# The first thirty microseconds of a fused conv and MLP kernel: longer TensorE warm-up, first input chunk in four transfers, later weight loads, one scaling on GpSimd

## The chip, the cores and the metric

The kernel runs on one NeuronCore of a Trainium2 chip. The metric is device time in microseconds (us), lower is better. Times are given as the median of several executions. One of them is profiled, and its span is about 1.7 us shorter than its time, because the profile counts from the first to the last instruction. Engines in the profile: PE is TensorE's matmul, PEld its weight load, DVE is VectorE, ACT is ScalarE, POOL is GpSimd, SP is the sync engine, which only issues transfers here.

## The reference

```python
# attention-like part: per head a causal convolution with 7 softmaxed taps
w = softmax(weight, axis=-1)                       # [8 heads, 7]
x_pad = concat([zeros(B, 6, D), x], axis=1)        # B=8, S=4096, D=192
conv[b, s, h, g] = sum_k w[h, k] * x_pad[b, s + k, h, g]
# MLP part, on 32768 tokens
h = conv @ w_in                                    # 192 -> 2048
g = h * sigmoid(beta * h)
out = g @ w_out                                    # 2048 -> 192
```

Inputs and output are float32. The kernel computes `silu(beta * h)` with `beta` as the activation's scale, and divides `w_out` by `beta` once at the start ("scaling of w_out").

## The kernel before

The tokens come in 32 stages of 2 x 512 tokens (two halves of the batch, `h = 0, 1`). In a stage, 16 blocks (`u`) each compute 128 hidden channels: six hidden matmuls, one silu on ACT, and output matmuls for earlier blocks. Chunk c's rows are loaded, cast to bf16, transposed so that channels lie on partitions, and convolved. For chunks 2 and on, the convolution runs on DVE and the transposes are DMAs. Chunk 0 is different: PE transposes it and convolves it with diagonal matrices (16 tap matmuls), because nothing else is ready yet. Chunk 1 is split between PE (`conv1`) and DVE.

The parts that the change touches (cuts marked with `...`):

```python
    def load_x(dst, t0):                      # two transfers of 384 KB, both h in each
        for i in range(2):
            t = t0 + i * 2 * BLK
            nc.sync.dma_start(
                out=dst[:, i].rearrange("q h b d -> q h (b d)"),
                in_=x_v[0, t : t + 2 * BLK, :, :].rearrange("(q b) h d -> q h (b d)", b=2))

    load_x(x0, 0)                             # chunk 0
    load_x(x1, TOK)                           # chunk 1
    for i in range(NW - 1):
        load_w_out(i)                         # w_out in quarters
    load(2); load_w_out(NW - 1); load(3)
    ...
    load_w_in(0)                              # w_in by quarters, GpSimd queue, cast to bf16 on the way
    ...
    def fill(n, cols=TOK):                    # matmuls of zeros: they only keep TensorE busy
        for _ in range(n):
            nc.tensor.matmul(pf[:, 0, 0:cols], zeros[:, 0:128], zeros[:, 0:cols], ...)

    fill(5)
    nc.tensor.matmul(pw, sel..., e8, ...)     # spreads the softmaxed taps over partitions
    fill(1, 384)
    for b in range(NB):                       # rows of chunk 0 to bf16, by token block
        cast_rows(nc.vector.tensor_copy, x0b, x0, b)
    ...
    hold = setup.tile([1, 1], BF16)           # GpSimd waits here for the first cast ...
    nc.gpsimd.tensor_copy(hold, x0b[0:1, 0, 0, 0, 0:1])
    for i in range(1, NW):
        load_w_in(i)                          # ... and issues the other w_in quarters then
    for b in range(NB):                       # PE transposes, ACT evacuates, fills between
        transposes(pt, x0b, b); nc.scalar.copy(tokens(xt0, b), pt)
        ...
    # diag = ident * cw (DVE); 16 diag taps (PE); 5 taps of the third channel group (DVE)
    ...
    CONV1 = {4: (0, 2), 5: (2, 4), 6: (4, 6), 7: (6, K)}   # chunk 1's PE taps in blocks 4..7
    first_work = {                            # DVE work of stage 0, by block; None = next conv step
        4: [None, lambda: scale_w_out(1), None],
        5: [None],
        7: [conv1_evac, lambda: scale_w_out(2), lambda: rows_of(2), None],
        8: [None, lambda: scale_w_out(3)],
        9: [None], 10: [None]}
```

`rows_of(2)` casts chunk 2's rows on DVE and starts their transposes. DVE works strictly in this order.

## Time and profile before

| | before |
|---|---|
| median, range (3 runs) | 693.16 us, 693.14 to 694.39 |
| profiled run: time, span | 692.46 us, 690.7 us |
| last row cast of chunk 0 ends | 6.13 us |
| first conv tap | 7.83 us |
| first silu | 14.31 us |
| second hidden block of stage 1 | 33.01 us |
| from there to the last hidden block, and to the end | 644.7 us, 13.1 us |

The second hidden block of stage 1 is a good marker. In every profile of this study except e7's and e9's (which move work into stage 1), the time from it to the start of the last stage (stage 31) is 626.29 to 626.31 us, and from there to the start of the last hidden block it is 18.37 to 18.38 us. Everything that differs lies before it or after the last hidden block.

From the page of the kernel before, its span and the busy time of the engines (busy us, share of the span, instructions):

```profile
span 690.7 us, 24335 instructions
PE 684.2 (99%) x11311; PEld 518.1 (75%) x11311; DVE 526.6 (76%) x466; ACT 579.1 (84%) x531; POOL 6.8 (1%) x18
```

PE is the limit of the whole. The reader should not conclude that the opening is also PE-bound. The timeline of the kernel before says otherwise. Its columns are start in us, length in us, engine, line, operation, output<-input, how many instructions were merged, and in brackets the idle time before and what ended it:

```profile
1.26 2.31 PE L228 MATMUL ph<-zeros 128*128 128x512 bf16 x5 [1.26 <-DVE warm L178]
...
4.29 0.74 DVE L233 CAST x0b<-x 128x384 bf16<-128x384 f32 x2 [1.78 <-DMA x<-in_x_dram]
...
5.35 0.78 DVE L233 CAST x0b<-x 128x384 bf16<-128x384 f32 x2 [0.32 <-DMA x<-in_x_dram]
...
7.83 3.04 PE L279 MATMUL ph<-xt,diag 128*128 128x512 f32 x7
...
10.71 1.79 PE L279 MATMUL pb<-xt,diag 128*128 128x512 f32 x7
...
14.31 6.45 ACT L425 ACTIVATE g<-ph,beta 128x1024 bf16<-128x1024 f32 x6
```

Seven taps took 3.04 us and the next seven 1.79 us. The same operation at two speeds is TensorE's clock. Single taps start about 427 ns apart up to the fifth interval (the first, 561 ns, excepted); the sixth is 378 ns, and from then on about 230 ns. The Trainium skill ("TensorE: Matmul & The Clock Gate", Part 1) describes a clock gate that lets half speed through until one free-running window of 3.4 us was busy, with 426.7 and 215.7 ns at N=512; the trace agrees with the first figure and shows about 230 ns for these fp32 taps. This trace holds no record of the first grant, so here the clock had to be read from the spacing.

The chain of waits of the kernel before, followed back from stage 1 (start us, length us, what ran; only the pieces that matter):

```profile
14.31 2.12 ACT g L425 x2
...
22.33 0.68 DVE ct L396
...
23.75 0.96 DVE w_out_s L313
24.71 1.20 DVE xb L106 x2
...
28.49 0.87 DVE w_out_s L313
29.35 1.21 DVE ct L335
...
30.59 1.29 DVE ct L335
...
31.92 0.61 PE ph L417 x4
```

From 22.33 us on the chain is DVE alone: conv1's evacuation, a scaling, chunk 2's casts, conv steps. PE waits for its end, at 31.92 us.

### The profile page before, as it was taken

What the parts mean: (1) busy time and instruction counts of PE and PEld (TensorE: products, weight loads), DVE (VectorE), ACT (ScalarE), POOL (GpSimd) and SP (SyncE); (2) the same over time, 40 slices, a digit from 0 to 9 for tenths busy, and PEclk for the clock granted to TensorE, in tenths of its full rate; (3) what the DMA queues carried; (4) which work ended last, traced back from release to release, by engine and by line L of the source; (5) the groups of instructions that cost most, each with busy time, mean ns of one, the idle gap of its engine ahead of it and who ended that gap; (6) DMA issues with size and microseconds to landing.
All of it is one profiled execution on the core that took longest, in us unless ns stands there. A gap on an engine that the chain in (4) does not pass through costs nothing.

```text
span 690.7 us, 24335 instructions
## 1 busy us (share of the span) xinstructions
PE 684.2 (99%) x11311; PEld 518.1 (75%) x11311; DVE 526.6 (76%) x466; ACT 579.1 (84%) x531; POOL 6.8 (1%) x18
## 2 busy tenths in 40 slices
PE   8999999999999999999999999999999999999997
PEld 4677777777777777777777777777777777777776
DVE  6888877797777797777887777887777977777712
ACT  6988888888888888888888888888888888888883
POOL 3000000000000000000000000000000000000000
DMA  9754332344332343332344332443323443322111
GB/s 214 176 117 116 93 104 69 85 116 112 92 104 58 102 116 104 97 95 61 109 116 105 93 83 70 116 116 92 104 56 98 116 106 98 98 60 60 48 37 59
DMA packets 121445, 66.86 MB, mean 97 GB/s; under 512 B 53232, under 2 KB 121344, under 8 KB 121344
## 3 DMA queue, kind: packets, MB, share of 16 engines
q1 hardware_dynamic: 119632, 63.73, 34.7%
q0 software_dynamic: 1664, 1.57, 1.4%
q8 instruction: 88, 1.44, 0.9%
q14 instruction: 13, 0.11, 0.1%
q10 hardware_dynamic: 48, 0.01, 0.0%
HBM read 29.89 MB, written 25.17 MB: 80 GB/s over the span
## 4 chain that ended last, share of the span: by engine, by line
PE 97%; DVE 1%; ACT 1%; issue 0%; ACTq 0%
PE ph L417 47%; PE pa L450 24%; PE pb L450 24%; DVE ct L335 1%; ACT g L425 0%; PE ph L279 0%; ACT x1b L233 0%; DVE w_out_s L313 0%; PE pb L279 0%; PE ph L228 0%; DVE ct L396 0%; DVE xb L106 0%; ACT ct L326 0%; PE pb L240 0%; PE ph L240 0%
## 5 line engine op out<-in xcount | busy, mean ns | idle before, releaser
L425 ACT ACTIVATE g<-ph,beta 128x1024 bf16<-128x1024 f32 x512 | 569.7, 1114 | 95.7 <-PE ph L417 89.6
L450 PEld LDWEIGHTS <-g 64*128 64x128 bf16 x8160 | 367.7, 94 | 106.3 <-ACT g L425 0.7
L417 PE MATMUL ph<-ct,w_in_s 64*128 64x512 bf16 x3072 | 422.8, 376 | 1.3 <-ACT g L425 0.9
L335 DVE SCALAR_TENSOR_TENSOR ct<-xt,cw,ct 128x1536 bf16<-128x1536 bf16 (+2 forms) x190 | 336.6, 1772 | 2.5
L450 PE MATMUL pa<-w_out_s,g 64*128 64x192 bf16 x4112 | 244.2, 243 | 0.6 <-ACT g L425 0.5
L450 PE MATMUL pb<-w_out_s,g 64*128 64x192 bf16 (+1 forms) x4048 | 229.7, 243 | 0.0
L417 PEld LDWEIGHTS <-w_in_s 64*128 64x128 bf16 x3072 | 156.7, 94 | 56.7 <-issue 3.4
L468 DVE TENSOR_REDUCE osb<-pa 128x384 f32<-128x768 f32 x64 | 61.3, 957 | 120.8 <-PE pa L450 119.9
L468 DVE TENSOR_REDUCE osb<-pb 128x384 f32<-128x768 f32 x63 | 60.3, 958 | 28.9 <-PE pb L450 28.8
L106 DVE CAST xb<-xf 128x768 bf16<-128x768 f32 x60 | 40.5, 677 | 0.0
L333 DVE TENSOR_SCALAR ct<-xt,cw 128x1536 bf16<-128x1536 bf16 (+2 forms) x32 | 31.1, 972 | 0.0
L466 ACT COPY osb<-pb 128x192 f32<-128x192 f32 x1 | 0.3, 318 | 6.7 <-PE pb L450 6.7
L228 PE MATMUL ph<-zeros 128*128 128x512 bf16 (+2 forms) x10 | 4.7, 551 | 1.3 <-DVE warm L178 1.3
L210 POOL DMA_DIRECT2D w_in_s<-in_moe_w_in_dram x8 | 5.2, 653 | 0.0
L279 PE MATMUL pb<-xt,diag 64*128 64x512 f32 (+1 forms) x21 | 4.7, 453 | 0.0
L313 DVE TENSOR_TENSOR w_out_s<-w_out_raw,beta_r 128x768 bf16<-128x768 f32 x4 | 3.8, 956 | 0.7 <-DMA w_out_raw<-in_moe_w_out_dram 0.6
L121 DVE COPY xt<-xt 128x18 bf16<-128x18 bf16 x27 | 4.3, 159 | 0.0
L326 ACT CAST ct<-ph 128x512 bf16<-128x512 f32 x1 | 0.6, 586 | 3.3 <-PE ph L279 3.3
L279 PEld LDWEIGHTS pb<-xt,diag 64*128 64x128 f32 (+1 forms) x21 | 2.7, 187 | 0.7
L279 PE MATMUL ph<-xt,diag 128*128 128x512 f32 x7 | 3.0, 603 | 0.1
L233 DVE CAST x0b<-x 128x384 bf16<-128x384 f32 x4 | 1.5, 420 | 2.1 <-DMA x<-in_x_dram 2.1
L228 PEld LDWEIGHTS <-zeros 128*128 128x128 bf16 x10 | 1.2, 133 | 2.1 <-DVE warm L178 1.3
(51 smaller groups left out, 27.7 us busy)
## 6 DMA issues: line engine op xcount, KB each, us to landing
out_dram<-osb SPq DMA_DIRECT2D x127, 192.0 KB, 2.1
xf<-in_x_dram SPq DMA_DIRECT2D x60, 384.0 KB, 4.1
xt<-xb SPq DMA_TRANSPOSE x120, 3.1
x<-in_x_dram SPq DMA_DIRECT2D x4, 384.0 KB, 4.6
w_in_s<-in_moe_w_in_dram POOLq DMA_DIRECT2D x8, 192.0 KB, 9.8
w_out_raw<-in_moe_w_out_dram SPq DMA_DIRECT2D x4, 384.0 KB, 14.6
out_dram<-osb SPq DMA_DIRECT2D x2, 96.0 KB, 1.6
cw<-in_weight_dram ACTq DMA_DIRECT2D x1, 0.2 KB
```

What stands on the lines that cost most here:

```text
L106: nc.vector.tensor_copy(xbs[ch][:, :, :, h, :], xfs[ch][:, h].rearrange("q b (p c) -> q b c p", c=NG),)
L121: nc.vector.tensor_copy(dst, last[:, :, HALO + TOK - PAD :])
L210: nc.gpsimd.dma_start(out=w_in_s[r * DG : (r + 1) * DG, :, cols], in_=w_in_v[:, :, cols])
L228: nc.tensor.matmul(pf[:, 0, 0:cols], zeros[:, 0:128], zeros[:, 0:cols], start=True, stop=True)
L279: nc.tensor.matmul(pv, diag[rows, k, :], xt[rows, o : o + TOK], start=(k == k0), stop=(k == K - 1),)
L313: nc.vector.tensor_tensor(w_out_s[:, fcs, :], w_out_raw[:, fcs, :], beta_r[:, fcs].unsqueeze(2).to_broadcast((128, NQ, D)), ALU.mult,)
L333: nc.vector.tensor_scalar_mul(dst, src, scalar)
L335: nc.vector.scalar_tensor_tensor(out=dst, in0=src, scalar=scalar, in1=dst, op0=ALU.mult, op1=ALU.add)
L417: nc.tensor.matmul(ph[:, h, :], w_in_s[rows, j, fc * 128 : (fc + 1) * 128], cts[s][rows, j, :], start=(j == 0), stop=(j == NG - 1),)
L425: nc.scalar.activation(gs[s][:, fc], ph, AF.Silu, scale=beta[:, fc : fc + 1])
L450: nc.tensor.matmul(self.po[:, r, b * D : (b + 1) * D], g[rows, fc, self.h, q * BLK : (q + 1) * BLK], w_out_s[rows, fc, :], start=(self.don ...
L468: nc.vector.tensor_reduce(dst, self.po[:, :, 0 : nb * D].rearrange("p r n -> p n r"), axis=mybir.AxisListType.X, op=ALU.add,)
```

## The change

The intent: let TensorE reach its full clock before the taps (eight unbroken fills, spread work between the transposes), get the first rows to the casts sooner (four transfers of 192 KB), keep w_in's later quarters away from the rows, and shorten DVE's chain (first w_out scaling on GpSimd, conv1 done one block earlier).

```diff
-    load_x(x0, 0)
+    for i in range(2):
+        for h in range(2):
+            nc.sync.dma_start(
+                out=x0[:, i, h].rearrange("q b d -> q (b d)"),
+                in_=x_v[0, i * 2 * BLK : (i + 1) * 2 * BLK, h, :].rearrange(
+                    "(q b) d -> q (b d)", b=2))
     load_x(x1, TOK)
...
-    zeros = setup.tile([128, TOK], BF16)
+    zeros = setup.tile([128, 128], BF16)          # fills broadcast it to N columns
...
-    fill(5)
-    nc.tensor.matmul(pw, sel..., e8, ...)
-    fill(1, 384)
-    for b in range(NB):
-        cast_rows(nc.vector.tensor_copy, x0b, x0, b)
-    (reciprocal, cw)
-    hold = ... nc.gpsimd.tensor_copy(hold, x0b[0:1, 0, 0, 0, 0:1])
-    for i in range(1, NW): load_w_in(i)
+    fill(8)
+    for i in range(2):                            # casts by transfer, not by block
+        for h in range(2):
+            nc.vector.tensor_copy(x0b[:, 2*i : 2*i+2, :, h, :], x0[:, i, h]...)
...
         if b == 0:
             fill(1, 256)
         elif b == 1:
-            fill(1, 384)
+            (pw matmul, reciprocal, cw); fill(1, 128)
+        elif b == 2:
+            fill(1, 128)
...
+    hold = ... nc.gpsimd.tensor_copy(hold, xt0[0:1, 0, HALO + TOK - 1 :]...)   # after the last ACT copy
+    for i in range(1, NW): load_w_in(i)
...
-        nc.vector.tensor_tensor(                  # in scale_w_out(i)
+        (nc.vector if i else nc.gpsimd).tensor_tensor(
...
-    CONV1 = {4: (0, 2), 5: (2, 4), 6: (4, 6), 7: (6, K)}
+    CONV1 = {4: (0, 2), 5: (2, 4), 6: (4, K)}
...
-        7: [conv1_evac, lambda: scale_w_out(2), lambda: rows_of(2), None],
+        6: [conv1_evac, lambda: scale_w_out(2), lambda: rows_of(2), None],
...
-    QUOTA_A = {3: 4, 7: 2}                        # output pairs in blocks 3..7 of stage 0
+    QUOTA_A = {4: 2, 7: 5}
...
-                output(s, u, 5 if u < NF - 1 else 8, "ab")
+                output(s, u, 5 if u < NF - 1 else 10, "ab")
```

More of the change, by code (lines that the diff above doesn't have):

```diff
@@ L165, in load_x @@
             )
-    load_x(x0, 0)
+    for i in range(2):
[3 more added lines that the diff above has]
+                in_=x_v[0, i * 2 * BLK : (i + 1) * 2 * BLK, h, :].rearrange(
+                    "(q b) d -> q (b d)", b=2
+                ),
+            )
     load_x(x1, TOK)
@@ L226, in fill @@
     def fill(n, cols=TOK):
+        zc = zeros.unsqueeze(1).to_broadcast((128, cols // 128, 128))
         for _ in range(n):
-            nc.tensor.matmul(
-                pf[:, 0, 0:cols], zeros[:, 0:128], zeros[:, 0:cols], start=True, stop=True
-            )
+            nc.tensor.matmul(pf[:, 0, 0:cols], zeros, zc, start=True, stop=True)
     def cast_rows(copy, xb, x, b):
@@ L251 @@
     rn = setup.tile([128, 1], FP32)
-    fill(5)
     pc = in_a()
     pw, pb = pc[:, 0, 0 : K + 1], pc[:, 1, 0:NF]
-    nc.tensor.matmul(
-        pw, sel.rearrange("i h p -> i (h p)"), e8, start=True, stop=True
-    )
-    fill(1, 384)
-    for b in range(NB):
-        cast_rows(nc.vector.tensor_copy, x0b, x0, b)
-    nc.vector.reciprocal(rn, pw[:, K : K + 1])
-    nc.vector.tensor_scalar_mul(cw, pw[:, 0:K], rn)
-    hold = setup.tile([1, 1], BF16)
-    nc.gpsimd.tensor_copy(hold, x0b[0:1, 0, 0, 0, 0:1])
-    for i in range(1, NW):
-        load_w_in(i)
+    fill(8)
+    for i in range(2):
+        for h in range(2):
+            nc.vector.tensor_copy(
+                x0b[:, 2 * i : 2 * i + 2, :, h, :],
+                x0[:, i, h].rearrange("q b (p c) -> q b c p", c=NG),
+            )
     diag = setup.tile([128, K, 128], FP32R)
@@ L297 @@
         elif b == 1:
-            fill(1, 384)
+            nc.tensor.matmul(
+                pw, sel.rearrange("i h p -> i (h p)"), e8, start=True, stop=True
+            )
+            nc.vector.reciprocal(rn, pw[:, K : K + 1])
+            nc.vector.tensor_scalar_mul(cw, pw[:, 0:K], rn)
+            fill(1, 128)
+        elif b == 2:
+            fill(1, 128)
     fill(1, 384)
     nc.tensor.transpose(pb, beta_q, ident[0:NF, 0:NF])
+    fill(1, 128)
     nc.scalar.copy(beta, pb)
-    fill(1, 256)
+    hold = setup.tile([1, 1], FP32)
+    nc.gpsimd.tensor_copy(hold, xt0[0:1, 0, HALO + TOK - 1 :].bitcast(FP32))
+    for i in range(1, NW):
+        load_w_in(i)
     for k0, k1 in ((0, 3), (3, K)):
```

## The prediction

> **What bounds the kernel now.** The page's engine table has PE busy 99% of the 690.7 us span, ACT 84%, DVE 76%. In the timeline every hidden block from 35 us on repeats each 1.307 us: six hidden and sixteen output matmuls back to back. So everything after about 32 us is TensorE-bound at full clock and untouched. The change can only move (a) when that steady part starts and (b) how many output pairs are left for the tail.
>
> **The opening of before, by the timeline and the chain of waits.** The chain runs: first warm-up; row casts (4.29 to 6.13 us); transposes and ACT copies (to 7.40); 16 conv taps (7.83 to 12.95); first hidden block (12.88); first silu at 14.31; sixteen silus of 1.08 us; conv1 evacuation on DVE (22.33); then an unbroken DVE chain to 31.87, for which PE waits 0.40 us in the first hidden block of stage 1. The clock: taps start 427 ns apart until about 10.35 us, then 230 ns. The Trainium skill ("TensorE: Matmul & The Clock Gate", Part 1) says half clock until one busy free-running window of about 3.4 us; 426.7 and 215.7 ns at N=512. The trace agrees, and shows that the broken warm-up (two idle gaps, transposes) didn't earn the clock before the taps.
>
> **What changes.**
> 1. Eight unbroken fills (8 x 427 ns, about 1.1 to 4.6 us). If full clock comes before 7.2 us, the taps take about 3.5 us instead of 5.1: up to -1.6 us. I give this 65%.
> 2. Four transfers: the same bytes at about 350 KB/us, so the last quarter still lands near 5.3 us, but one cast follows it, not two (0.37 us): rows and diag about 0.3 us earlier.
> 3. The first w_out scaling leaves DVE: 0.96 us plus a 0.62 us DMA wait. On GpSimd I estimate 1.9 us (the skill, "GPSIMD Engine Reference", 3.1, has its two-input op 1.96 times DVE's); no run shows it yet. The first output pair moves to u=4, so it should just fit.
> 4. conv1 finishes one block (1.08 us) earlier.
> 5. The w_in remainder is issued about 7.3 us, not 5.0; slices arrive 1 to 2 us later, still in time.
> 6. 52 output pairs in stage 0, not 49: 3 x 82 ns = -0.25 us in the tail.
>
> First silu: 14.31 to about 12.7 us (other limits there: five DVE taps, 3.6 us, and w_in's first slice, landed at 12.0).
>
> **How much counts.** Less than it looks. The DMA engines are 99% busy from 4 to 25 us; the second w_out quarter landed at 18.2 us and chunk 2's rows at 23.2 and 24.3 (DMA issues, time to landing). The bytes before those rows are unchanged. DVE casts them inside its in-order chain, and 6.3 us of work follow. So that chain can't end before about 24.3 + 0.6 + 6.3 = 31.2 us, whatever the clock does; before it ended at 31.9. I expect PE to wait over 1 us at the start of stage 1. Gain: 0.3 to 0.7 us there, 0.25 in the tail, and some more against the median because the profiled run (692.5) was a lucky one.
>
> **Prediction: 692.0 us, range 690.8 to 693.1; faster by over 2%: 0.5%, within 2%: 99%, slower: 0.5%.**
>
> **Signs.** Right: first silu before 13.3 us; tap spacing near 230 ns from the first tap; DVE waiting on DMA for w_out or chunk 2's rows between 16 and 25 us; a PE wait over 0.8 us on DVE near 31 us; 1.307 us blocks unchanged. Wrong: taps still 427 ns apart; chunk 2's rows landing before 23.5 us (then the gain is nearer 2.5 us, 690.6).
>
> **What would break it.** GpSimd scaling over 3 us or holding DVE back; w_in slices late at u=4; a clock window in another phase.

## The result, and the profile after

Ratios in this document are the mean time of one kernel's fast runs over the mean of the other's fast runs of the same rounds, so they are not quite the ratio of the medians.

| | before | after |
|---|---|---|
| median, range (4 runs each) | 693.15 us, 692.95 to 694.39 | 694.65 us, 693.93 to 695.40 |
| ratio to before, 95% interval | | 1.0018, 1.0001 to 1.0035 |
| profiled run: time, span | 692.46, 690.7 us | 695.08, 693.4 us |
| last row cast of chunk 0 ends | 6.13 us | 8.47 us |
| first tap; 16th tap starts | 7.83; 12.56 us | 10.05; 15.57 us |
| first silu | 14.31 us | 17.25 us |
| second hidden block of stage 1 | 33.01 us | 35.48 us |
| last hidden block to the end | 13.07 us | 13.22 us |

The changed kernel is slower, by 1.5 us in the medians and 2.6 us in the two profiled runs. By the 2% rule this is "same"; in the opening it is a clear loss.

The page of the changed kernel:

```profile
span 693.4 us, 24343 instructions
PE 684.3 (99%) x11314; PEld 536.8 (77%) x11314; DVE 523.2 (75%) x465; ACT 578.9 (83%) x531; POOL 8.3 (1%) x19
...
PEclk8999999999999999999999999999999999999999
```

The span grew while PE's busy time stayed at 684 us, and a clock row has appeared whose first slice is 0.8. So TensorE was idle and slow at the start. The timeline of the changed kernel, the lines that answer to those of before:

```profile
1.06 3.36 PE L237 MATMUL ph<-zeros 128*128 128x512 bf16 x8 [1.06 <-DVE warm L185]
...
3.22 0.41 DVE L265 CAST x0b<-x 128x384 bf16<-128x384 f32 x1 [0.22 <-DMA x<-in_x_dram]
...
3.95 0.42 DVE L265 CAST x0b<-x 128x384 bf16<-128x384 f32 x1 [0.31 <-DMA x<-in_x_dram]
...
5.69 0.41 DVE L265 CAST x0b<-x 128x384 bf16<-128x384 f32 x1 [1.32 <-DMA x<-in_x_dram]
...
8.05 0.42 DVE L265 CAST x0b<-x 128x384 bf16<-128x384 f32 x1 [1.95 <-DMA x<-in_x_dram]
...
8.53 0.50 PE L247 MATMUL pb<-ident_b,x0b 128*128 128x128 bf16 x3 [3.01 <-DVE x0b L265]
...
10.05 3.35 PE L279 MATMUL ph<-xt,diag 128*128 128x512 f32 x7
...
13.20 2.29 PE L279 MATMUL pb<-xt,diag 128*128 128x512 f32 x7
```

Quarters one and two came early, as intended (3.22 and 3.95 us). Quarter three came at 5.69 us and quarter four at 8.05 us, where both halves had been in by 5.35 us before. TensorE stood idle for 3.01 us. The granted clock, from the table by stretches of the changed kernel (us from the start, length, busy us and instructions of each engine, granted clock, DMA share, GB/s):

```profile
core 0: us, PE busy (x) PEld busy (x) DVE busy (x) ACT busy (x) POOL busy (x), PEclk, DMA share, GB/s
0.00:4.05 4.05, 2.99 (x8) 1.04 (x8) 1.08 (x7) 2.23 (x5) 2.95 (x11) 1.00 0.48 135
4.05:7.46 3.41, 1.47 (x12) 0.82 (x10) 0.73 (x2) 1.78 (x4) 0.00 (x0) 1.00 0.91 209
7.46:10.88 3.42, 2.35 (x12) 1.79 (x13) 2.69 (x7) 1.10 (x3) 0.82 (x3) 0.50 1.09 291
10.88:14.29 3.41, 3.41 (x9) 2.64 (x9) 2.68 (x4) 0.85 (x2) 3.02 (x5) 0.50 1.11 336
14.29:20.00 5.71, 4.83 (x55) 2.73 (x55) 3.24 (x9) 5.42 (x8) 1.47 (x1) 1.00 1.19 231
```

The warm-up worked. The trace's clock record begins with full clock at 4.05 us, as the last of the eight fills starts. (The 1.00 of the first stretch only means that no record covers it: the fills start 427 ns apart.) But the window after it was busy for 1.47 of 3.41 us, and at 7.46 us the clock fell back to half, for two windows, just before the taps came. Nine intervals between taps were slow (about 427 ns, the first one longer), where five were slow before.

The chain of waits of the changed kernel names the same culprit:

```profile
2.20 5.83 DMA x<-in_x_dram
8.05 0.43 DVE x0b L265
8.53 0.50 PE pb L247 x3
...
10.21 3.19 PE ph L279 x7
13.40 2.10 PE pb L279 x7
15.53 0.59 ACT ct L340
16.12 1.09 ACT x1b L240 x2
17.25 3.15 ACT g L439 x3
```

A transfer issued at 2.20 us took 5.83 us. DVE's conv chain no longer appears in it.

The difference in span, 2.62 us, adds up from the two traces:

| step | cost |
|---|---|
| last row cast later (8.47 - 6.13) | +2.34 us |
| 16 taps, first start to last start (5.52 - 4.73), the lost clock | +0.79 us |
| rest up to the first silu | -0.19 us |
| first silu to second block of stage 1 (18.23 - 18.70) | -0.47 us |
| after the last hidden block (13.22 - 13.07) | +0.15 us |

So the part behind the first silu gained 0.47 us. That it began later, and so found more of its data landed, is not the reason: e3 below keeps the old arrangement behind a first silu almost as late (16.97 us) and takes 18.77 us to the second block of stage 1. The opening in front of it lost six times as much.

### The profile page after: what moved, and what is told of

It reads as the page before. It is cut to its first block, busy times and chain, and to the rows that moved or that the text cites. A ratio compares the mean times of both kernels' runs of the same rounds, so it can differ in the third digit from the quotient of the medians.

```text
span 693.4 us, 24343 instructions
## 1 busy us (share of the span) xinstructions
PE 684.3 (99%) x11314; PEld 536.8 (77%) x11314; DVE 523.2 (75%) x465; ACT 578.9 (83%) x531; POOL 8.3 (1%) x19
## 3 DMA queue, kind: packets, MB, share of 16 engines
q0 software_dynamic: 1664, 1.57, 1.4%
## 4 chain that ended last, share of the span: by engine, by line
PE 97%; ACT 1%; DMA 1%; SPq 0%; issue 0%; DVE 0%
PE ph L431 47%; PE pa L464 25%; PE pb L464 24%; DMA x<-in_x_dram 1%; ACT g L439 1%; PE pb L279 1%; PE ph L279 0%; SPq L169 0%; ACT x1b L240 0%; PE ph L237 0%; ACT ct L340 0%; PE pb L247 0%; DVE x0b L265 0%; PE ph L247 0%; ACT osb L480 0%
## 5 line engine op out<-in xcount | busy, mean ns | idle before, releaser
L464 PEld LDWEIGHTS <-g 64*128 64x128 bf16 x8160 | 379.8, 94 | 93.8 <-ACT g L439 0.7
L431 PE MATMUL ph<-ct,w_in_s 64*128 64x512 bf16 x3072 | 428.7, 376 | 1.1 <-ACT g L439 1.1
L464 PE MATMUL pa<-w_out_s,g 64*128 64x192 bf16 x4112 | 249.5, 243 | 0.5 <-ACT g L439 0.5
L464 PE MATMUL pb<-w_out_s,g 64*128 64x192 bf16 (+1 forms) x4048 | 233.8, 243 | 0.0
L431 PEld LDWEIGHTS <-w_in_s 64*128 64x128 bf16 x3072 | 168.9, 94 | 50.4 <-issue 2.9
L237 PE MATMUL ph<-zeros 128*128 128x512 bf16 (+3 forms) x13 | 5.0, 494 | 1.1 <-DVE warm L185 1.1
```

The lines of the kernel that those rows point to most:

```text
L237: nc.tensor.matmul(pf[:, 0, 0:cols], zeros, zc, start=True, stop=True)
L431: nc.tensor.matmul(ph[:, h, :], w_in_s[rows, j, fc * 128 : (fc + 1) * 128], cts[s][rows, j, :], start=(j == 0), stop=(j == NG - 1),)
L464: nc.tensor.matmul(self.po[:, r, b * D : (b + 1) * D], g[rows, fc, self.h, q * BLK : (q + 1) * BLK], w_out_s[rows, fc, :], start=(self.don ...
```

## The experiments

Two theories stood at the start. A: cutting chunk 0 into four transfers is what makes its second half late; the idle time and the lost clock follow. B: the number of transfers is innocent; w_in's first quarter, whose packets began at 4.47 us in the trace and at 5.67 us before, is what slows the rows. There was also N: the first profile was one bad execution. Later the question was what limits the opening once the rows are in time.

### e1: the changed kernel again

No edit.

> The changed kernel unchanged, a second profile and five more rounds. Theory A (the four transfers let the last quarter of chunk 0 land late, TensorE stands idle and its clock falls back) and theory B (the first w_in slice, whose packets began at 4.5 us and not 5.7, is what delays the rows) both expect the same picture as in the first profile: fourth quarter after 7 us, a TensorE gap over 2 us before the third transposes, taps 427 ns apart. If the first profile was one bad execution (theory N), the fourth quarter lands near 5.3 us here.

Measured: 694.43 us (693.45 to 695.41, 5 runs), ratio 1.002, interval 1.0006 to 1.0034. Last two casts at 5.82 and 7.45 us, first silu 16.61 us, nine slow taps. Here the fills never earned the clock at all (first grant in the record: 13.63 us), as the windows lay differently: counted back from 13.63 us in steps of 3.41 us, a boundary falls at 3.39 us, in the midst of the fills. N is out, and the loss is the late rows in both profiles.

### e2: the changed kernel with two transfers

```diff
-    for i in range(2):
-        for h in range(2):
-            nc.sync.dma_start(out=x0[:, i, h]..., in_=x_v[0, ..., h, :]...)
+    load_x(x0, 0)
```

> The changed kernel with chunk 0 loaded in two transfers, as before; all else of the change kept. A: rows of the second half land near 5.3 us, TensorE idles under 1 us, the clock stays granted, taps about 230 ns apart, first silu near 12.8 us (17.25 in the changed kernel), time at least 2 us under the changed kernel, about 691 to 692 us. B: rows still land after 7 us and the time stays at 694 to 695.

Measured: 692.19 us (691.65 to 692.57, 5 runs), ratio to before 0.9986, interval 0.9974 to 0.9999. The timeline of DVE:

```profile
4.33 0.74 DVE L258 CAST x0b<-x 128x384 bf16<-128x384 f32 x2 [1.84 <-DMA x<-in_x_dram]
5.35 0.74 DVE L258 CAST x0b<-x 128x384 bf16<-128x384 f32 x2 [0.28 <-DMA x<-in_x_dram]
```

All casts end at 6.09 us, the clock is granted at 4.69 us and kept, taps are about 230 ns apart (the first interval, 342 ns, excepted), first silu at 13.54 us. Undoing the four transfers alone turns the loss into a gain of 0.9 us over before. A predicts this; B, as it was put down, does not. But w_in's first packet moved too, to 6.12 us, so a weaker B is left to e4.

### e3: the kernel before with four transfers

```diff
-    load_x(x0, 0)
+    (the four transfers of the change)
...
-    for b in range(NB):
-        cast_rows(nc.vector.tensor_copy, x0b, x0, b)
+    (the four casts of the change)
```

> The kernel before with only the four transfers and the casts by quarter. A: the last quarter lands after 7 us, first silu about 2 to 3 us later than 14.3, time 1.5 to 3 us over the kernel before. B: the order of the loads alone costs nothing unless w_in's first packets also move earlier; rows near 5.3 us and time within 0.5 us of before.

Measured: 695.59 us (695.21 to 697.33, 5 runs), ratio 1.0045, interval 1.0031 to 1.0059. Casts at 3.30, 4.20, 5.91 and 7.71 us, first silu 16.97 us. The cost shows in the other kernel too: about 2.5 us in the medians. B expected no cost unless w_in's packets also moved forward; they did (4.48 us against 5.67), so e3 alone does not part A from B.

### e4: the changed kernel with w_in's first quarter behind the rows

```diff
+    hold0 = setup.tile([1, 1], FP32)
+    nc.gpsimd.tensor_copy(hold0, x0[0:1, 1, 1, 0, 0:1])   # waits for quarter four
     load_w_in(0)
```

> The changed kernel with the first w_in slice issued only when the fourth quarter of chunk 0 has landed. If w_in's packets are what slows the quarters (B, or A with this as its means), the four quarters land by 5.4 us and TensorE idles under 1 us; the slice itself then lands near 12 us or later and holds the first hidden block. If the four transfers are slow in themselves, the fourth quarter still lands after 7 us.

Measured: 695.64 us (695.12 to 696.97, 4 runs), ratio 1.0041, interval 1.0027 to 1.0054. w_in's first packet came at 10.19 us, so it could not disturb. Quarter three still landed at 5.72 us, and quarter four at 6.22 us. So neither expectation was met whole. As far as one profile tells, w_in's traffic accounts for 1.2 to 1.8 us of quarter four (7.42 and 8.03 us in e1 and the first profile), and none of quarter three's delay; the rest is there without it. The time is worse because w_in then arrives too late for the first hidden block (first silu 18.13 us).

### e5: two transfers, cut by half of the batch

```diff
+    for h in range(2):
+        nc.sync.dma_start(
+            out=x0[:, :, h].rearrange("q i b d -> q i (b d)"),
+            in_=x_v[0, 0:TOK, h, :].rearrange("(i q b) d -> q i (b d)", i=2, b=2))
```

> The changed kernel with chunk 0 in two transfers of 384 KB, cut by the half of the batch (h) and not by token block, so that the same contiguous source regions are read as by the four. If the source layout (one h at a time) makes quarters three and four slow, the second transfer lands after 6 us. If it is the number and size of the transfers, it lands near 5.3 us, TensorE stays warm, and the time is within 0.5 us of the two-transfer version (692.2), a little later at the first transposes because both transfers are needed for any block.

Measured: 692.20 us (692.11 to 692.31, 4 runs), ratio 0.9985, interval 0.9972 to 0.9999. Transfers landed by 4.1 and 5.2 us. The source order is not it; the number and size of the transfers on the one queue are left (e12 narrows this further). This run gave one thing more. In its profile the clock was lost again (at 8.05 us, a window with PE busy 2.28 of 3.41 us), eight tap intervals were slow, and the first silu came at 14.75 us, 1.2 us later than in e2. Yet the second block of stage 1 came at 33.05 us, against 32.98 us in e2. So at this level the clock during the taps made no difference to the start of stage 1; something else set it.

### e6: four transfers from two queues, first try

```diff
-            nc.sync.dma_start(          # chunk 0's quarters
+            (nc.scalar if h else nc.sync).dma_start(
...
-    nc.scalar.dma_start(out=cw8, in_=weight); nc.scalar.dma_start(out=beta_q, ...)
+    nc.sync.dma_start(out=cw8, in_=weight); nc.sync.dma_start(out=beta_q, ...)    # after the quarters
```

> The changed kernel with its four transfers, two of them issued by ScalarE's queue, so that all four are issued by 1.7 us and not by 2.6 us (weight and beta go after them on the sync queue). If the rows are late because 192 KB transfers are issued too slowly on one queue, all four quarters land by about 5.3 us and the time comes near 692. If not, quarter four stays over 6.5 us and the time near 694.5.

Measured: 694.60 us (694.36 to 694.91, 4 runs), ratio 1.0019, interval 1.0003 to 1.0034. All four quarters landed by 5.42 us, as the issue-rate reading expects. But the time did not follow, by a fault of the experiment: the weight load, moved behind the quarters, landed at 5.65 us, and DVE, in order, first computed the softmax's maximum, so the casts began at 5.88 us. Confounded; e12 mends it.

### e7: two transfers, chunk 2's rows behind the conv steps

```diff
-        6: [conv1_evac, lambda: scale_w_out(2), lambda: rows_of(2), None],
+        6: [conv1_evac, None, lambda: scale_w_out(2)],
         8: [None, lambda: scale_w_out(3)],
-        9: [None], 10: [None],
+        9: [None], 10: [None, lambda: rows_of(2)],
```

> The two-transfer version, with the casts and transposes of chunk 2's rows moved behind the last conv step of chunk 1 on VectorE, and the third w_out scaling behind the next conv step. If, as predicted, the start of stage 1 hangs on VectorE's chain behind chunk 2's rows (cast at 24.3 us, chain end 31.8 us), the chain now ends near 29.5 us, the first hidden block of stage 1 starts near 30.5 us (31.7 there) and the time falls by 0.8 to 1.4 us, to about 691.0. If the start of stage 1 is set by ScalarE's silus alone, nothing changes (692.2).

Measured: 692.88 us (692.41 to 693.48, 5 runs), ratio 0.9994, interval 0.9982 to 1.0007. DVE's chain did end earlier, 30.05 us against 31.83, but the second block of stage 1 came at 32.95 us, as in e2 (32.98). So the chain behind chunk 2's rows was not the limit of e2, and the reason that the prediction gave for a small gain was not the one at work. The chain of waits of e2 shows what was:

```profile
8.32 9.67 DMA w_in_s<-in_moe_w_in_dram
17.99 0.05 issue
18.04 0.69 PE ph L424 x5
```

The second half of w_in's second quarter, issued at 8.32 us because GpSimd is held until the last ACT copy, landed at 17.99 us (17.86 in e7). In e2 the first matmul of the block that uses it, u = 4, ran at 16.73 us, the other five from 18.04. From there the chain of e2 is PE alone, into stage 1. That the median is 0.7 us above e2's is partly a new wait: in e7's profile one block near the end of stage 1 takes 1.57 us and not 1.31 (1.55 in e9's, which shares the edit); I did not follow that up.

### e8: four transfers, but TensorE kept busy

```diff
             (pw matmul, reciprocal, cw)
-            fill(1, 128)
+            fill(12)
```

> The changed kernel with twelve more fills of N=512 behind the second block's transposes, so that TensorE is busy while quarters three and four arrive. The rows should still be late (cast of quarter four ending near 8 us) but the clock not fall back: the first nine taps 230 ns apart and not 427, which is 1.7 us. Expect first silu near 15.2 us (17.25 in the changed kernel) and time 1.0 to 1.8 us under it, near 693. If the lost clock is not what costs, the time stays at 694.5.

Measured: 693.00 us (692.86 to 694.11, 4 runs), ratio 1.0, interval 0.9987 to 1.0014. The rows were as late as ever (last cast ends 8.23 us), the clock stayed granted from 3.73 us on, the taps were about 230 ns apart (the first interval, 334 ns, excepted), and the first silu came at 14.96 us. The first seven taps, 3.35 us in the changed kernel:

```profile
9.62 1.90 PE L279 MATMUL ph<-xt,diag 128*128 128x512 f32 x7 [0.28 <-ACT beta L309]
```

This parts the two costs: holding the clock, with the rows still late, takes 1.65 us off the changed kernel's median, or 1.2 us by the two ratios to before (1.0018 and 1.0).

### e9 and e10: w_in issued early again

In both, w_in's later quarters are issued after the first row cast, as in the kernel before. e9 is e7 with that, e10 is e2 with that.

```diff
+    hold = setup.tile([1, 1], BF16)
+    nc.gpsimd.tensor_copy(hold, x0b[0:1, 0, 0, 0, 0:1])
+    for i in range(1, NW): load_w_in(i)
...
-    hold = ... nc.gpsimd.tensor_copy(hold, xt0[0:1, 0, HALO + TOK - 1 :]...)
-    for i in range(1, NW): load_w_in(i)
```

> The two-transfer version with chunk 2's rows behind the conv steps and, new, the remaining w_in slices issued after the first row cast as in the kernel before (near 5 us and not 7.7 us). If the fast opening is stopped by two limits at once, w_in's second slice (landed 17.9 us, wanted at 16.7) and VectorE's chain behind chunk 2's rows (end 31.8 us), then with both taken away the fourth hidden block no longer waits for a DMA, silus are 1.0 to 1.1 us apart throughout, stage 1 starts near 30.5 us (31.6), and the time is 691.0 to 691.5, 1.5 us or more under the kernel before of the same rounds. If w_in is not a limit, no gain over the version without it (692.2 to 692.9).

> The two-transfer version with the early issue of w_in alone; chunk 2's rows stay where the change has them. The wait for w_in at the fourth block goes, but VectorE's chain still ends near 31.3 to 31.9 us, behind chunk 2's rows: stage 1 starts near 31.5 us and the time stays within 0.4 us of the two-transfer version (692.2). If the chain is no limit, the time is near 691.2.

Measured: e9 692.19 us (692.02 to 692.26, 5 runs), ratio 0.9990, interval 0.9977 to 1.0002. e10 692.02 us (691.20 to 692.24, 5 runs), ratio 0.9985, interval 0.9972 to 0.9997. In both the wait for w_in at block u = 4 is gone (silus 1.02 us apart there, 2.31 in e2). In e10's profile stage 1's second block comes at 31.99 us, a full microsecond before e2's, and now DVE is what PE waits for:

```profile
29.56 1.30 DVE ct L342
30.86 0.04 issue
30.90 0.61 PE ph L424 x4
```

So the predicted limit exists, one step behind the w_in one. That profile is of e10's fastest run, though; its median is only 0.2 us below e2's. In e9's profile the clock was lost after a window with PE busy 2.52 of 3.41 us, the first silu came at 14.40 us, and with both named limits gone the start of stage 1 followed the silus again (32.70 us). The expected 691.0 to 691.5 was missed.

### e11: two transfers, first scaling back on VectorE

```diff
-        (nc.vector if i else nc.gpsimd).tensor_tensor(
+        nc.vector.tensor_tensor(
```

> The two-transfer version with the first w_out scaling back on VectorE. If the GpSimd scaling is worth something or harms, the time moves; by my account it lies off the limiting path (VectorE waits for landings later in its chain anyway): within 0.3 us of 692.2, VectorE's chain end within 0.5 us of 31.8.

Measured: 692.10 us (690.94 to 692.23, 4 runs), ratio 0.9985, interval 0.9972 to 0.9999. The GpSimd scaling (1.47 us there, 0.96 us on DVE) makes no difference that these runs resolve. DVE's chain in the profile ended at 30.60 us, 1.2 us earlier than in e2's, outside what I had expected, in that kernel's fastest run.

### e12 and e13: four transfers from two queues, mended and repeated

The weight load stays first on ScalarE's queue; only beta moves to the sync queue. e13 is the same kernel.

```diff
+            (nc.scalar if h else nc.sync).dma_start(    # chunk 0's quarters
...
-    nc.scalar.dma_start(out=beta_q, ...)
+    nc.sync.dma_start(out=beta_q, ...)                  # after the quarters
```

> The earlier try with two queues for the four transfers, mended: the weight load goes first on ScalarE's queue again, so that no cast waits for it; only beta moves to the sync queue. All four quarters issued by 2.3 us. If the issue rate of one queue makes quarters three and four late, all casts end by 5.9 us, TensorE does not idle over 1 us, and the time is near 692.2. If it is the transfer count itself, quarter four's cast starts after 6.5 us and the time stays near 694.5.

> The mended two-queue kernel once more, unchanged. Its rows came in time (casts end 5.68 us, first tap 7.34 us, stage 1 at 33.0 us, all as in the two-transfer version), but its span was 1.2 us longer, all of it after the last matmul (4.21 us to the end, 3.08 there). If that end is a fluke of one chip or profile, the end is now 3.0 to 3.5 us and the time 692.2 to 692.7; if it belongs to this kernel, again near 4.2 us and 693.4.

Measured: e12 693.40 us (693.04 to 694.50, 4 runs), ratio 1.0011, interval 0.9996 to 1.0026. e13 694.26 us (693.20 to 695.07, 5 runs), ratio 1.0017, interval 1.0005 to 1.0030. DVE's timeline in e12:

```profile
3.25 0.51 DVE L265 CAST x0b<-x 128x384 bf16<-128x384 f32 x1 [0.76 <-DMA x<-in_x_dram]
4.61 1.08 DVE L265 CAST x0b<-x 128x384 bf16<-128x384 f32 x3 [0.85 <-DMA x<-in_x_dram]
```

The rows are in time with four transfers, all casts end by 5.69 us in both profiles, the clock is kept, and the second block of stage 1 comes at 33.04 and 33.11 us, as in e2. So four transfers are not late in themselves; four transfers issued one after the other by one queue are. These runs do not part the slower issue of one queue from the mere presence of a second one: in e12 the last quarter was issued only 0.38 us sooner than in the changed kernel (1.82 against 2.20 us), and landed 2.93 us sooner (5.10 against 8.03). The time did not come back with them: in both profiles the end, after the last matmul, is 4.21 and 3.88 us long (3.08 in e2), because the last output lands 2.15 and 1.83 us after it is issued, not 1.28 us as before; the rest is the order of the final waits (e14). It came in both profiles, so it is no single fluke. It explains about 1 us; e13's median is 1 us further above its own profiled run, and no profile shows where.

### e14: two more transfers, far from the opening

```diff
-    load_w_out(NW - 1)
+    (the same load in three transfers)
```

> The two-transfer version with the last w_out load, far from the opening, cut in three, so that the program has as many transfers on this queue as the changed kernel. In all six profiles of kernels with two more transfers the last matmul lies 3.46 us or more before the end, in the others 3.08 us: at the end the sync queue waits for its semaphores in a fixed order, 0.065 us each, and in the former the one that comes last stands second and not eighth. If that is the reason, 3.46 us here and the time 0.4 us over the two-transfer version (about 692.6); opening unchanged. If it is the four transfers of chunk 0, 3.08 us.

Measured: 692.43 us (691.87 to 693.89, 5 runs), ratio 0.9996, interval 0.9983 to 1.0008. Last matmul to the end: 3.47 us, with chunk 0 in two transfers. At the end of the program the sync queue waits for its transfer semaphores in a fixed order. These are the starts of its last waits in the raw trace, in us from the end:

```
before:  -2.31  -2.24  -2.18  -2.11  -2.05  -1.99  -1.93  [last landing -1.08]  -1.06  -1.00   then drains
e14:     -2.70  [last landing -1.45]  -1.44  -1.37  -1.31  -1.24  -1.18  -1.12  -1.06  -1.00   then drains
```

With two transfers more, the last output uses another semaphore, which is waited for second and not eighth, and six waits of 0.065 us then follow the landing. That is 0.39 us, and the changed kernel has it too (3.47 us). It ate the predicted 0.25 us of the tail.

### e15: what the runs pointed to, together

Two transfers, casts by token block, w_in early, conv steps before chunk 2's casts, longer fills between the transposes. On top of e9:

```diff
-    (four casts by i and h)
+    for b in range(NB): cast_rows(nc.vector.tensor_copy, x0b, x0, b)
...
-            fill(1, 256)      # after block 0       +            fill(1)
-            fill(1, 128)      # after block 1       +            fill(2)
-    fill(1, 384)              # after the last      +    fill(2)
...
-        9: [None], 10: [None, lambda: rows_of(2)],
+        9: [None, lambda: cast(2, 0)], 10: [None, lambda: cast(2, 1), lambda: xpose(2)],
```

> What the runs point to, together: two transfers, casts by token block as in the kernel before, the other w_in slices issued at 5 us, the conv steps of chunk 1 ahead of the casts of chunk 2 on VectorE, and longer fills between the transposes so that a window after the grant is not too idle. With both limits gone: first silu 13.0 to 13.6 us, silus 1.0 to 1.1 us apart from the sixth on, stage 1 (second block) near 31.5 us (33.0 before in its profile), time 690.9 to 691.5, under every kernel so far. If the time stays at 692.0 to 692.3, a limit is left that I have not named.

Measured: 692.46 us (691.94 to 692.48, 5 runs), ratio 0.9990, interval 0.9977 to 1.0004. Missed. The clock was kept (granted at 4.77 us, PE busy 3.38 of 3.41 us in the next window) and w_in was in time, but a third limit stood behind the two:

```profile
25.85 0.34 PE L453 MATMUL pa<-w_out_s,g 64*128 64x192 bf16 x4 [0.81 <-DVE w_out_s L316]
```

Since e7 the third w_out scaling stands one conv step later on DVE. In e9 that was just in time: the scaling ended at 25.22 us and the matmuls that need it ran at 25.27. Here the second quarter of w_out landed 0.58 us later (18.81 us, 18.23 in e9), the scalings behind it came late, the third one ended at 25.79 us, and output matmuls in the eleventh block (u = 10), which the kept clock had brought forward, waited.

### e16: the kernel before, profiled again

No edit; one run.

> The kernel before, for a second profile, because the first fell in a fast execution (692.46 us; median 693.15). If its runs differ by the phase of the clock's windows, the taps here turn fast at another tap than the seventh, and the second hidden block of stage 1 starts by the same amount later or earlier than 33.01 us.

Measured: 692.93 us, span 691.2 us (one run, so its state is unknown). The clock came at 11.63 us, at the ninth tap interval and not the sixth; first silu 14.94 us, second block of stage 1 at 33.49 us. The first profile was a fast one by about half a microsecond of opening.

## Why the prediction was right or wrong

**The step that failed** is the second: "the same bytes at about 350 KB/us, so the last quarter still lands near 5.3 us". It landed at 8.03 us. I had costed the transfers by their bytes and a rate, and not asked whether one queue could keep that rate up with smaller transfers. In the kernel before, the sync queue starts a 384 KB transfer every 0.51 us; with 192 KB it starts one every 0.46 us. My estimate from these (bytes over interval, 1 KB = 1,024 bytes) is 770 and 427 GB/s offered, against 297 to 387 GB/s, 361 on average, that the kernel before moved in the quarter-microseconds from 3 to 5 us. The margin shrank from twofold to a fifth. The intervals are a quarter of these issue times (four loads each, before and after):

```profile
0.81 2.01 SPq L160 DMA_DIRECT2D x<-in_x_dram  x4
0.81 1.82 SPq L169 DMA_DIRECT2D x<-in_x_dram  x4
```

But 427 is still more than 361, so this sum alone does not make the engines wait. The traces show where the bytes went missing. From 3.25 to 4.25 us, before w_in's first packet (4.47 us) and after all four quarters had been issued (by 2.63 us), the DMA engines moved half of what they moved before, at a lower busy share; with two queues they did not. These are before, changed and e12, in the columns of the table by stretches (the last two are DMA share and GB/s):

```profile
3.25:4.25 1.00, 0.84 (x4) 0.53 (x3) 0.00 (x0) 0.98 (x4) 0.31 (x1) 1.00 0.98 356
3.25:4.25 1.00, 1.00 (x4) 0.23 (x2) 0.69 (x2) 0.98 (x4) 0.52 (x1) 1.00 0.81 179
3.25:4.25 1.00, 1.00 (x4) 0.23 (x2) 0.51 (x1) 0.97 (x5) 0.35 (x1) 1.00 1.09 377
```

e4, with w_in's packets far away, shows the same dip (0.81, 204 GB/s), so w_in does not start it. What is shown, then: four loads of 192 KB from one queue come late, from two queues in time (e6, e12, e13); the source order is not the cause (e5), and w_in only part of it (e4). That the issue rate of one queue is the reason is argued and fits; why the engines slackened with loads already issued, and so what happens inside them, is not shown. The Trainium skill ("DMA: Bandwidth & Descriptors", Queues, rings and completion order) says that each DMA engine round-robins, packet by packet, between the queue rows it has work for; w_in's packets starting 1.2 us sooner beside the thinner stream would fit that, for the part of quarter four's delay that went with w_in in e4, but no run parts it from other causes.

**The clock.** The mechanism was right: unbroken fills earned it at 4.05 us in the profiled run (though not in e1). The 65% was not wrong about earning it but did not think of losing it. A window with TensorE busy for 1.47 of 3.41 us took it back. e8 puts a price on that: 1.2 us by the ratios, 1.65 us by the medians, about all of the loss against before. How little work loses the clock is not settled: in e4 a window with 2.08 us of transposes and short fills lost it, and a later one with 1.96 us, mostly of matmuls with 512 columns, kept it. (The 0.79 us in the table of steps is less, because the kernel before had slow taps too.) In e8 the late rows are still there, and the clock and the other gains just make up for them.

**Most of it lies off the critical path.** In its direction this was right: e2, the change without the four transfers, came out at 692.19 us, where I had predicted 692.0 for the whole, and e5's 1.2 us later silu cost nothing. That the two numbers are so close is partly luck, for the reason was only partly right. I named DVE's chain behind chunk 2's rows; e7 took it away and nothing moved. The first limit was w_in's second quarter. The prediction's fifth point, "slices arrive 1 to 2 us later, still in time", was the miss: in e2 it landed at 17.99 us, 1.2 us too late. In the changed kernel itself it was in time (18.46 us), because everything else was later still. e10 shows DVE's chain as the next limit, e15 the w_out scalings as one more (one profile each). All hang on transfers that keep the DMA engines full until 25 us.

**GpSimd scaling.** Estimated 1.9 us, from the Trainium skill's 1.96 ("GPSIMD Engine Reference", 3.1); measured 1.47 us against 0.96, a factor of 1.53. It did just fit, and e11 finds it worth nothing.

**conv1 earlier, DVE's chain off the path.** Right: first silu to the second block of stage 1 fell from 18.70 to 18.23 us, and PE no longer waits for DVE there; no run tests conv1's move alone. The predicted PE wait over 0.8 us at stage 1 did not show, because the late opening made the silus last.

**The tail.** Six matmuls fewer did leave less work; the time from the last hidden block to the last matmul fell from 9.99 to 9.75 us. The two added transfers gave 0.39 us back in the final semaphore waits (e14). I had not counted them.

**Open.** Why e13's other runs are up to 2 us over its profile; why the last output lands later in e12 and e13; what slows quarter three where w_in is out of the way; whether it is the issue rate of one queue or the lack of a second queue that makes the quarters late.

**The best version.** e2, e5, e10 and e11 are all near 692.1 us, 0.15% under before with intervals that just exclude 1, and e2 is 2.2 us under the changed kernel run beside it (e1). These runs do not tell them apart.

## What to carry to other kernels

Cutting a load to get its first part sooner also lowers what each issue offers. Compare the bytes per issue interval of one queue with the rate at which the engines drain it (a test that fits these runs, not a proven rule); if they are close, try two queues or don't cut. A warm-up can be lost in the very next window, as here: what follows must keep TensorE at work, or fills that wait for nothing must stand in for it (twelve of 512 columns in e8). And when many things load at once, removing one late arrival uncovers the next, so expect less than the sum of the waits.

## What the Trainium skill lacked or had wrong

- "DMA: Bandwidth & Descriptors": its closing table says that spreading loads over issuing engines "only saves sequencer issue time". Here spreading mattered by more than that: four 192 KB loads issued 0.46 us apart by one queue landed by 8.03 us, four from two queues by 5.1 us (e12), although the last of them was issued only 0.38 us sooner; the engines moved 179 and 377 GB/s from 3.25 to 4.25 us. Two loads of 384 KB from one queue landed by 5.33 us (e2).
- "TensorE: Matmul & The Clock Gate": it says how long an idle stretch loses the clock (about 3 us, one window). It gives no busy share, and the profile's busy time gives none here. In e4 a window with PE busy 2.08 of 3.41 us (4.71 to 8.12 us: transposes and short fills, longest idle stretch 1.05 us) lost it, and one with 1.96 us (14.95 to 18.36 us: mostly matmuls of 512 columns, an idle stretch of 1.18 us) kept it; 2.52 us did both (e9 lost, e10 kept). Nor does busy time decide the earning: windows with 2.67 (e8), 2.89 (e7) and 2.99 us (the changed kernel) earned it, 2.86 (e1) and 3.18 us (e16) did not. The idle stretch at the start of e5's lost window was 1.0 us (4.66 to 5.66 us).
- "GPSIMD Engine Reference", 3.1: the two-input factor of 1.96 was 1.53 here (1.47 against 0.96 us for a multiplication of 128x768, one input float32, one broadcast, output bf16). The page's case is another, a float32 addition of 2,048 elements, so this adds a case and corrects nothing.
- No page that I read has the order of the final semaphore waits: 0.065 us each behind the last landing, 0.39 us more or less by the number of transfers in the program (e14).
